# Keys of the first four tiles from LN(x)·(1 + scale), the shift added later as a bias, with a new load order and a new written order

## The chip, the cores and the metric

The kernel runs on one core of one Trainium2 chip. That core has TensorE (PE in the profile, with its weight loads listed as PEld), VectorE (DVE), ScalarE (ACT), GpSimd (POOL) and the SyncE queue (SP), which here issues nearly all transfers; 16 DMA engines carry them. The metric is device microseconds (us) of one execution, and lower is better. The kernel before took 242.55 us, the median of three runs (242.29 to 243.35).

## The reference

One transformer block on x, 2048 rows of 512 numbers in bf16. Each of its two layers takes a layernorm that is scaled and shifted by vectors computed from a conditioning row c:

```
mod = (silu(c) @ w_mod).reshape(1, 6, 1, 512)     # sa, ca, ga, sb, cb, gb
h = layernorm(x) * (1 + ca) + sa
q, k, v = h @ wqkv                                # 32 heads of 16
# each row s attends to rows s, s-2, ..., s-14 (8 keys, softmax over them)
x = x + ga * (attention @ wo)
h = layernorm(x) * (1 + cb) + sb
x = x + gb * ((silu(h @ w1) * (h @ w3)) @ w2)     # F = 1792
```

w_mod is 512 x 3072, so its first 512 columns give the shift sa and the next 512 the scale ca.

## The kernel before, in words

**Tiles.** x is cut into 16 tiles of 128 rows, tile T holding rows 128T to 128T+127, on 128 partitions. The first layer works on groups of tiles, `LN1 = [[0, 1], [2, 3], [4, 5, 6, 7], [8, 9, 10, 11], [12, 13, 14, 15]]` (L276). For each group `ln_stats` (L535 and on) takes mean and variance of each tile on DVE (`bn_stats`, L542, and `bn_aggr`, L543), the reciprocal root on POOL (L547, L549), and the normalized tile xn on DVE (L554). `ln_T` turns the tiles over, so that features lie on partitions: by PE transposes (L614) into PSUM for the first four groups, by a transposing DMA for the last. On the way out of PSUM, ACT (L622), or DVE for two of the first group's four pieces (L629), applies the modulation: times column `modc[:, 4 + ft]`, plus column `modc[:, ft]`. The result h (128 features x rows, four pieces ft) feeds `proj_qk` (L666, evicted by ACT at L674 for q and L675 for k) and `proj_v` (L685, evicted at L695). v goes out to DRAM and comes back gathered (`vsh`), four transfers of 256 KB a tile.

**Modulation.** `modulation(0)` computes shift and scale together: tanh of c (L456, ACT), two DVE operations that make silu(c) (L458, L460), a PE transpose (L462), a DVE copy into `csz` (L464), then 32 small matmuls (L480) in four parts, one for each 128-row piece of w_mod (256 KB each), and a DVE copy into `modc` (L491). Dummy matmuls of 512 columns (`warm`, L502) stand in between: `WARMS = (8, 3, 3, 4, 2)`, 20 in all.

**Attention and FFN.** For each tile, DVE multiplies q with eight shifted keys (L716, one instruction of 4096 elements a partition), PE sums heads (L725), DVE and ACT take the softmax, DVE multiplies gathered values with the weights (L800), PE sums them (L809) and applies wo (L833), DVE adds the residual (L837). The second layernorm takes its sums on ACT (L568, L579), and the FFN runs on PE (L849, L880, L892) with ACT and DVE behind it. FFN groups are `FFN = [[0,1],[2,3],[4,5,6,7],[8,9,10,11],[12,13],[14,15]]`.

**What sets the order.** Every operation is recorded with its engine, reads and writes. Two long lists written out by hand or by a search, ORDER and SLOTS, fix the sequence on each engine and the buffer of each pooled value. Each engine runs its list strictly in sequence and waits where an operation needs another engine's result or a buffer that is still in use. No scheduler decides anything at run time, so an instruction that waits holds up all that stand behind it on its engine. SP's list is the order of the loads:

```
for T in range(2):
    p.dma(x_sb[:, T, :], x_view[:, T, :], ("load", 1), (128, 1024), w=[vx[T]])
for t in range(KT):
    p.dma(wm_s[0][:, t, :], wm_view[:, t, 0:1024], ("load", 2), (128, 2048), w=[vwm0[t]], again=WMOD)
p.dma(x_sb[:, 2:4, :], x_view[:, 2:4, :], ("load", 27), (256, 1024), w=vx[2:4])
```

In ORDER the queue begins x0, x1, the four w_mod pieces, the k part of wqkv, x2-3, the q part, x4-7, the v part, x8-11, x12-15.

Of the kernel before, what the change touches and what calls it, by code (L numbers as in the profile page):

```python
# [10 lines left out]
P = 128  # L11
S = 2048
D = 512
# [254 lines left out]
WMOD = 120  # L268
WARMS = (8, 3, 3, 4, 2)
NVB = 6  # L270
NOB = 4
DMA_T = (4, 2)
# [3 lines left out]
LN1 = [[0, 1], [2, 3], [4, 5, 6, 7], [8, 9, 10, 11], [12, 13, 14, 15]]  # L276


def _build(p, A_x, A_wqkv, A_wo, B_w1, B_w3, B_w2, c, w_mod, out):
# [46 lines left out]
    modc = sb([P, 16], f32, "modc")  # L326
    mbase = sb([P, 8], bf, "mbase")
# [96 lines left out]
    vwq = [Val("wq"), Val("wk"), Val("wv")]  # L424
    wqkv_view = A_wqkv.rearrange("(t p) n -> p t n", p=P)
    for i in range(3):
# [23 lines left out]
    for g in range(NG):  # L450
# [13 lines left out]
    p.op("dve", lambda e: e.tensor_copy(csz[:, :, 7], bank(vpc).bitcast(bf)[:, 0:KT]), 180, ("mod", 1), r=[vpc, vcsz], w=[vcs])  # L464

    vmod = [Val("modA"), Val("modB")]
    vg = [Val("ga"), Val("gb")]

    def modulation(i):
        k = ("mod", 2 + i)  # L470
        vm = Val("ps_mod", psum)
        jlo = 8 * i

        def mm(e, ts):
            b = bank(vm)
            if ts[0] == 0:
                e.matmul(b[:, 0:8], ident[:], mbase[:], start=True, stop=False)
            for t in ts:
                for j in range(8):
                    ins = e.matmul(b[:, 0:8], wm_s[i][:, t, j * P:(j + 1) * P], csz[:, t, 7 - j:15 - j], start=False,  # L480
# [3 lines left out]
        o = None  # L484
        for ts in ([(t,) for t in range(KT)] if i == 0 else [tuple(range(KT))]):
            after = warm(WARMS[ts[0]]) if i == 0 else []
            o = p.op("pe", lambda e, ts=ts: mm(e, ts), (8 * len(ts) + (ts[0] == 0)) * 27, k,
                     r=[vwms[1]] * i + [vwm0[t] for t in ts] * (1 - i) + [vcs, vident, vbase] + wm_hold, part=[vm],
                     after=after + ([o] if o else []))
            last[0] = o  # L490
# [558 lines left out]
```

## Time and profile before

| what | value |
|---|---|
| median of three runs | 242.55 us |
| the profiled execution | 242.59 us, of which the span is 240.6 us |
| PE busy | 232.7 us, 97% of the span |
| DVE busy | 168.3 us, 70% |
| ACT busy | 157.9 us, 66% |
| first matmul of a projection (L666) | 10.42 us |
| first large DVE product (L716) | 23.35 us |
| moved by DMA | 38.33 MB, mean 159 GB/s |

Times in the profile count from the start of the span. In a group's or timeline's row, the first figures are start and length (or busy time and mean length), then engine, line, operation, output and inputs, number of instructions, and in brackets the idle time before and what ended it. In the view by stretch, each row has the stretch, its length, the busy time of PE, PEld, DVE, ACT and POOL with numbers of instructions, the granted clock, the share of the 16 DMA engines and GB/s. A busy PE counts matmuls whose ends are modelled, so the distance from one matmul's start to the next says more than the busy time. Several helpers record operations on one line; the line then stands for all uses, and the tile names tell them apart.

### The profile page before, as it was taken

How to read it: one execution, taken by the hardware profiler on the slowest of the kernel's cores; microseconds unless marked ns; L12 is line 12 of the kernel's file. 1: busy time of each engine (PE TensorE's matmuls, PEld its weight loads, DVE VectorE, ACT ScalarE, POOL GpSimd, SP SyncE). 2: the span in 40 equal slices, each digit the busy share in tenths (PEclk: the TensorE clock that was granted, in tenths of full speed). 3: DMA queues.
4: the chain of work that ended last, by engine and by line, in shares of the span. 5: the costliest groups of instructions: out<-in, count | busy, mean ns of one | idle time of the engine just before them, and what ended most of it. 6: DMA issues, size and time to landing. Idle time of an engine off the chain costs nothing.

```text
span 240.6 us, 4592 instructions
## 1 busy us (share of the span) xinstructions
PE 232.7 (97%) x1794; PEld 136.3 (57%) x1820; DVE 168.3 (70%) x287; ACT 157.9 (66%) x329; POOL 21.1 (9%) x54
## 2 busy tenths in 40 slices
PE   7989999999999999999999999999999999999995
PEld 2557644545577867664444444444474447576774
DVE  4489999999999999999999658335453224152352
ACT  2169687988999888768858988746754583422310
POOL 4254110000001000130000110001000100000000
DMA  6997999699499959696875963454302000301011
GB/s 191 354 321 226 284 227 248 188 289 346 131 243 270 280 163 226 183 315 101 236 184 166 204 196 75 100 152 45 89 15 52 3 0 3 85 24 65 3 44 45
DMA packets 44125, 38.33 MB, mean 159 GB/s; under 512 B 19512, under 2 KB 34888, under 8 KB 44104
## 3 DMA queue, kind: packets, MB, share of 16 engines
q1 hardware_dynamic: 44096, 38.04, 59.5%
q8 instruction: 14, 0.23, 0.4%
q14 instruction: 7, 0.06, 0.1%
q10 hardware_dynamic: 8, 0.00, 0.0%
HBM read 29.62 MB, written 4.21 MB: 141 GB/s over the span
## 4 chain that ended last, share of the span: by engine, by line
PE 79%; DMA 7%; ACT 5%; DVE 3%; SPq 2%; issue 2%; POOL 1%
PE pall L849 32%; PE pall L892 14%; PE pall L666 10%; PE pall L833 5%; PE pall L685 4%; DMA sb_w<-in_B_w_dram 4%; PE pall L809 3%; PE pall L725 3%; PE pall L502 3%; PE pall L880 3%; SPq L124 2%; DMA sb_h<-sb_xn 2%; DMA out_dram<-sb_o 2%; PE pall L614 1%; ACT sb_h L622 1%
## 5 line engine op out<-in xcount | busy, mean ns | idle before, releaser
L849 PE MATMUL pall<-sb_h,sb_w 128*128 128x256 bf16 (+1 forms) x666 | 102.5, 308 | 1.1 <-ACT sb_hh L859 0.4
L849 PEld LDWEIGHTS pall<-sb_h,sb_w 128*128 128x128 bf16 x672 | 64.7, 98 | 37.3 <-ACT sb_hh L859 1.5
L855 ACT ACTIVATE sb_sg<-pall 128x256 bf16<-128x256 f32 (+1 forms) x84 | 36.5, 457 | 33.3 <-PE pall L849 29.4
L892 PE MATMUL pall<-sb_w,sb_hh 128*128 128x512 bf16 x189 | 43.4, 379 | 0.6 <-issue 0.3
L716 DVE TENSOR_TENSOR sb_pq<-sb_q,sb_kT 128x4096 bf16<-128x4096 bf16 x16 | 36.5, 2283 | 0.0
L666 PE MATMUL pall<-sb_h,sb_wqkv 128*128 128x512 bf16 (+1 forms) x156 | 30.9, 336 | 1.1 <-ACT sb_h L622 0.5
L892 PEld LDWEIGHTS pall<-sb_w,sb_hh 128*128 128x128 bf16 x196 | 19.0, 98 | 21.4 <-issue 0.4
L859 ACT ACTIVATE sb_hh<-pall 128x256 bf16<-128x256 f32 (+1 forms) x56 | 26.3, 491 | 6.9 <-PE pall L849 6.7
L800 DVE TENSOR_TENSOR sb_vsh<-sb_vsh,sb_al 128x4096 bf16<-128x4096 bf16 x13 | 29.5, 2285 | 0.4 <-ACT sb_al L784 0.4
L908 DVE TENSOR_TENSOR sb_o<-pall,sb_x 128x512 bf16<-128x512 f32 (+1 forms) x18 | 11.1, 626 | 22.4 <-PE pall L892 14.3
L860 DVE TENSOR_TENSOR sb_hh<-sb_sg,sb_hh 128x256 bf16<-128x256 bf16 (+1 forms) x56 | 18.4, 352 | 11.4 <-ACT sb_hh L859 7.6
L666 PEld LDWEIGHTS pall<-sb_h,sb_wqkv 128*128 128x128 bf16 x160 | 14.6, 98 | 12.7 <-ACT sb_h L622 0.9
L863 DVE TENSOR_TENSOR sb_hh<-sb_sg,pall 128x256 bf16<-128x256 bf16 x28 | 10.9, 416 | 12.8 <-PE pall L849 11.4
L622 ACT ACTIVATE sb_h<-pall,sb_modc 128x256 bf16<-128x256 bf16 (+1 forms) x22 | 13.2, 673 | 8.8 <-DVE sb_modc L491 7.0
L574 POOL TENSOR_SCALAR sb_rs<-sb_var 128x2 f32<-128x2 f32 x8 | 3.5, 434 | 151.4 <-ACT sb_xn L568 151.4
L833 PE MATMUL pall<-sb_wo,sb_ot 128*128 128x512 bf16 x61 | 15.5, 380 | 0.3 <-issue 0.2
L599 ACT ACTIVATE sb_h<-sb_h,sb_modc 128x512 bf16<-128x512 bf16 (+1 forms) x20 | 13.2, 723 | 3.3 <-DMA sb_h<-sb_xn 3.3
L685 PE MATMUL pall<-sb_wqkv,sb_h 128*128 128x512 bf16 x59 | 15.0, 380 | 0.4 <-issue 0.2
L568 ACT ACTIVATE sb_xn<-sb_x,sb_nm 128x512 bf16<-128x512 bf16 x16 | 11.4, 714 | 5.9 <-DVE sb_nm L564 5.9
L579 ACT ACTIVATE sb_xn<-sb_x,sb_nb,sb_rs 128x512 bf16<-128x512 bf16 x16 | 12.7, 810 | 3.4 <-DVE sb_nb L576 3.4
L837 DVE SCALAR_TENSOR_TENSOR sb_x<-pall,sb_x 128x512 bf16<-128x512 f32 x16 | 10.9, 687 | 2.7 <-PE pall L833 2.6
L675 ACT ACTIVATE sb_kT<-pall 128x512 bf16<-128x512 f32 (+1 forms) x20 | 9.8, 519 | 3.5 <-PE pall L666 3.5
(84 smaller groups left out, 222.1 us busy)
## 6 DMA issues: line engine op xcount, KB each, us to landing
sb_vsh<-v_scratch_dram SPq DMA_DIRECT2D x52, 256.0 KB, 4.6
sb_w<-in_B_w_dram SPq DMA_DIRECT2D x6, 512.0 KB, 7.3
sb_vshx<-v_scratch_dram SPq DMA_DIRECT2D x12, 256.0 KB, 4.6
sb_w<-in_B_w_dram SPq DMA_DIRECT2D x6, 384.0 KB, 5.6
v_scratch_dram<-sb_v SPq DMA_DIRECT2D x16, 128.0 KB, 3.9
out_dram<-sb_o SPq DMA_DIRECT2D x14, 128.0 KB, 1.9
sb_wqkv<-in_A_wqkv_dram SPq DMA_DIRECT2D x3, 512.0 KB, 7.0
sb_x<-in_A_x_dram SPq DMA_DIRECT2D x3, 512.0 KB, 8.8
```

What stands on the lines that cost most here:

```text
L599: return e.activation(vh.at[:, ft, 0:n * P], vh.at[:, ft, 0:n * P], ACT.Identity, bias=modc[:, 8 * which + ft:8 * which + ft + 1], scale=m ...
L622: return e.activation(vh.at[:, ft, 0:n * P], b[:, j * 512:j * 512 + n * P], ACT.Identity, bias=modc[:, 8 * which + ft:8 * which + ft + 1], ...
L666: ins = e.matmul(bank(vp)[:, 0:n], wqkv[:, t, kind * D + ft * P:kind * D + (ft + 1) * P], vh.at[:, t, 0:n], start=(t == ORDER[0]), stop=(t ...
L685: ins = e.matmul(bank(vp), vh.at[:, t, tt * P:(tt + 1) * P], wqkv[:, t, 2 * D:3 * D], start=(t == ORDER[0]), stop=(t == ORDER[-1]))
L716: return e.tensor_tensor(vp.at[:], in0, in1, ALU.mult)
L800: return e.tensor_tensor(v_w, v_w, a_w, ALU.mult)
L833: ins = e.matmul(bank(vy), vt.at[:, ft, :], wo[:, ft, :], start=(ft == 0), stop=(ft == KT - 1))
L849: ins = e.matmul(bank(vp)[:, 0:n], wt[:, t, fi * P:(fi + 1) * P], vh.at[:, t, 0:n], start=(t == 0), stop=(t == KT - 1))
L855: p.op("act", lambda e: e.activation(vt.at[:, 0:n], bank(vgp)[:, 0:n], ACT.Silu), c_act(n), k, r=[vgp], w=[vt], table="silu")
L859: p.op("act", lambda e: e.activation(vh_.at[:, 0:n], bank(vup)[:, 0:n], ACT.Copy), c_act(n), k, r=[vup], w=[vh_])
L860: p.op("dve", lambda e: e.tensor_tensor(vh_.at[:, 0:n], vt.at[:, 0:n], vh_.at[:, 0:n], ALU.mult), 60 + n * 69 // 128, k, r=[vt], w=[vh_], ...
L892: ins = e.matmul(bank(vz), vhh[fi].at[:, tt * P:(tt + 1) * P], w2[:, fi, :], start=(fi == 0), stop=(fi == NF - 1))
```

## The change

The shift is separated from the scale for tiles 0 to 3. With hs = LN(x)·(1 + ca), the keys are (hs + sa) @ Wk = hs @ Wk + sa @ Wk, so k is computed from hs, and the column kb = sa @ Wk is added when k leaves PSUM. q and v still use hs + sa, which DVE adds before them. In parts:

- Tiles 0 to 3 are one group. `first_keys` evicts their transposes times the scale only (ACT two pieces, DVE two, for each pair of tiles), and computes k in four PSUM banks of 512 columns: tiles 0-1 piece by piece, then tiles 2-3. q of the four tiles takes matmuls of 512 columns in place of 256.
- `scales` uses the scale half of the first w_mod piece alone (17 small matmuls in place of 33). `shifts` computes sa from the shift half (16 matmuls of one column), copies it twice, and computes kb (16 more and one copy).
- Silu(c) moves from DVE to two POOL operations, and the csz copy from DVE to ACT.
- Tile 3's mean and variance come from two ACT passes and two tiny DVE operations (`moments`). The addition of epsilon for tiles 0 and 1 moves from POOL to DVE.
- SP loads x0, x1, x2, x3 (128 KB each), the four scale pieces (128 KB each), wk in two halves, the shift half (512 KB), wq, x4-7, wv, x8-11, x12-15. Later loads have another order too: the w_o quarters go behind both gate halves, one FFN piece goes ahead of them.
- `DMA_T` counts groups, so its new value leaves tiles 12 to 15 on the transposing DMA as before.
- Dummy matmuls go from 20 to 14. ORDER and SLOTS are new throughout, so the sequence of attention and FFN on every engine differs from before as well.

```diff
-WMOD = 120
-WARMS = (8, 3, 3, 4, 2)
+WMOD = 66
+WARMS = (8, 1, 1, 1, 3)
-DMA_T = (4, 2)
+DMA_T = (3, 2)
+KEV = (0, 1, 2, 3)
+STACT = (3,)
-LN1 = [[0, 1], [2, 3], [4, 5, 6, 7], [8, 9, 10, 11], [12, 13, 14, 15]]
+LN1 = [[0, 1, 2, 3], [4, 5, 6, 7], [8, 9, 10, 11], [12, 13, 14, 15]]
...
-    for T in range(2):
+    for T in range(4):
         p.dma(x_sb[:, T, :], x_view[:, T, :], ("load", 1), (128, 1024), w=[vx[T]])
...
-        p.dma(wm_s[0][:, t, :], wm_view[:, t, 0:1024], ("load", 2), (128, 2048), w=[vwm0[t]], again=WMOD)
-    p.dma(x_sb[:, 2:4, :], x_view[:, 2:4, :], ("load", 27), (256, 1024), w=vx[2:4])
+        p.dma(wm_s[0][:, t, D:2 * D], wm_view[:, t, D:2 * D], ("load", 2), (128, 1024), w=[vwm0[t]], again=WMOD)
...
+    for i in range(2):
+        p.dma(wqkv[:, i::2, D:2 * D], wqkv_view[:, i::2, D:2 * D], ("load", 4), (256, 1024), w=[vwq[1][i]])
+    vwsa = Val("wms0_sa")
+    p.dma(wm_s[0][:, :, 0:D], wm_view[:, :, 0:D], ("load", 28), (512, 1024), w=[vwsa])
...
-    p.op("dve", lambda e: e.scalar_tensor_tensor(c4s[:], thc[:], 1.0, c4[:], op0=ALU.add, op1=ALU.mult), 180, k,
-         r=[vthc, vcT], w=[vc4])
-    p.op("dve", lambda e: e.tensor_scalar(c4s[:], c4s[:], 0.5, None, op0=ALU.mult), 180, k, w=[vc4])
+    p.op("pool", lambda e: e.tensor_scalar(thc[:], thc[:], 1.0, None, op0=ALU.add), 250, k, w=[vthc])
+    p.op("pool", lambda e: e.tensor_tensor(c4s[:], thc[:], c4[:], ALU.mult), 300, k, r=[vthc, vcT], w=[vc4])
...
-    p.op("dve", lambda e: e.tensor_copy(csz[:, :, 7], bank(vpc).bitcast(bf)[:, 0:KT]), 180, ("mod", 1), r=[vpc, vcsz], w=[vcs])
+    p.op("act", lambda e: e.activation(csz[:, :, 7], bank(vpc).bitcast(bf)[:, 0:KT], ACT.Copy, scale=0.5), 180, ("mod", 1),
+         r=[vpc, vcsz], w=[vcs])
...
+        p.op("pe", lambda e: columns(e, vm, wm_s[0], lambda t: csz[:, t, 7:8]), 16 * 27, k, r=[vwsa, vcs] + wm_hold, w=[vm])
+        p.op("dve", lambda e: e.tensor_copy(sab[:], bank(vm)[:, 0:KT]), 100, k, r=[vm], w=[vsab])
+        p.op("dve", lambda e: e.tensor_copy(modc[:, 0:4], bank(vm)[:, 0:KT]), 100, k, r=[vm], w=[vsa])
+        p.op("pe", lambda e: columns(e, vb, wqkv[:, :, D:2 * D], lambda t: sab[:, t:t + 1]), 16 * 27, ("mod", 12),
+             r=[vsab] + vwq[1] + qkv_hold, w=[vb])
+        p.op("dve", lambda e: e.tensor_copy(kb[:], bank(vb)[:, 0:KT]), 100, ("mod", 12), r=[vb], w=[vkb])
...
+    def moments(T):
...
+        p.op("act", lambda e: e.activation(vn.at[:], x_sb[:, T, :], ACT.Identity, accum_out=sx[:, T, :]), c_act(512) + 212, k,
+             r=[vx[T]], w=[vs, vn])
+        p.op("dve", lambda e: e.tensor_scalar(nm[:, T, :], sx[:, T, :], -D ** -1.5, None, op0=ALU.mult), C_TINY, k, r=[vs], w=[vb])
+        p.op("act", lambda e: e.activation(vn.at[:], x_sb[:, T, :], ACT.Square, bias=nm[:, T, :], scale=D ** -0.5,
+                                           accum_out=mv[:, T, 1:2]), c_act(512) + 212, k, r=[vx[T], vb], w=[vv, vn])
...
+    def first_keys(vnss):
...
+                        if half:
+                            return e.tensor_scalar(vo.at[:, ft, c0:c0 + n], src, sc, None, op0=ALU.mult)
+                        return e.activation(vo.at[:, ft, c0:c0 + n], src, ACT.Copy, scale=sc)
...
+                if ft in KEV:
+                    return e.activation(dst, bank(vps[ft]), ACT.Identity, bias=kb[:, ft:ft + 1])
...
+        for ft in ORDER:
+            def add(e, ft=ft):
+                return e.tensor_scalar(vh.at[:, ft, :], vo.at[:, ft, :], modc[:, ft:ft + 1], None, op0=ALU.add)
...
-    modulation(0)
+    scales()
     warm(WARMS[4])
+    shifts()
     for gi, Ts in enumerate(LN1):
-        vns = [v for pr in ([[T] for T in Ts] if gi == 0 else pairs(Ts)) for v in ln_stats(pr)]
-        vh = ln_T(0, gi, vns)
+        if gi == 0:
+            vh = first_keys([[v for T in (0, 1) for v in ln_stats([T])], ln_stats([2, 3])])
+        else:
+            vh = ln_T(0, gi, [v for pr in pairs(Ts) for v in ln_stats(pr)])
```

More of the change, by code (lines that the diff above doesn't have):

```diff
@@ L481, in mm @@
                                    stop=(t == KT - 1 and j == 7))
             return ins
[L484 to L490, printed above, removed]
@@ L588, in ln_T @@
         vh = Val("h", hpool)
-        vh.pieces = [Val(f"h_{ft}") for ft in range(KT)] if not which and not gi else None
+        vh.pieces = None
+        k0 = 2 * (gi + 1) if not which else 2 * gi + 2 * len(LN1) + 2
+        modv = [vmodB] if which else [vca, vsa]
         n = len(vns)
         if gi >= DMA_T[which]:
-            k = ("tr", 2 * gi + (2 * len(LN1) if which else 0))
+            k = ("tr", k0)
             vt = Val("hT")
@@ L923, in _build @@
          ("mod", 6), r=[vwo, vg[0]], w=[vsc_wo], lock=True)
-    modulation(1)
+    modulation()
     gate(1)
```

145 lines of the change are left out of this document (110 added, 35 removed), and 128 rows, old and new, of tables (ORDER, SLOTS).

## The prediction

> **What bounds the kernel now.** I read the page's busy times, then the busy times by stretch, then the start of the chain of waits, then the order of time around the first projections and around the multiplication with the values. All figures are us unless marked.
>
> ```profile
> PE 232.7 (97%) x1794; PEld 136.3 (57%) x1820; DVE 168.3 (70%) x287; ACT 157.9 (66%) x329; POOL 21.1 (9%) x54
> ```
>
> ```profile
> 0.00:10.42 10.42, 8.61 (x61) 3.71 (x63) 4.22 (x13) 2.06 (x4) 4.24 (x21) 1.00 0.80 260
> ...
> 14.00:22.00 8.00, 7.50 (x71) 5.88 (x74) 8.00 (x25) 6.57 (x17) 4.20 (x10) 1.00 0.89 251
> 22.00:30.00 8.00, 7.79 (x103) 4.82 (x103) 8.00 (x15) 5.67 (x11) 1.09 (x3) 1.00 1.02 285
> 30.00:62.00 32.00, 31.68 (x297) 16.03 (x299) 31.80 (x33) 27.50 (x52) 1.85 (x4) 1.00 0.94 257
> 62.00:78.70 16.70, 16.32 (x155) 11.44 (x150) 16.21 (x25) 15.97 (x39) 0.99 (x2) 1.00 0.85 220
> 78.70:110.00 31.30, 30.98 (x289) 21.33 (x294) 30.25 (x53) 24.70 (x63) 3.55 (x4) 1.00 0.89 225
> 110.00:158.00 48.00, 47.42 (x297) 22.00 (x300) 37.20 (x55) 37.84 (x64) 1.85 (x4) 1.00 0.63 154
> ```
>
> TensorE (PE) is busy nearly always, so time can only come from the stretch before its first useful matmul. But from 14 to 110 VectorE (the third figure behind the length) works 94.3 of 96: a second bound, and an earlier PE helps only as far as DVE follows. The chain names what holds the start:
>
> ```profile
> 8.94 0.59 PE pall L502 x2
> 9.53 0.20 PE pall L480 x8
> 9.75 0.18 DVE sb_modc L491
> 9.95 0.73 DVE sb_h L629 x2
> ```
>
> ```profile
> 10.42 3.16 PE L666 MATMUL pall<-sb_h,sb_wqkv 128*128 128x256 bf16 x26 [0.26 <-DVE sb_h L629]
> ```
>
> Dummy matmuls (L502), the modulation (L480), its copy (L491), the first h (L629): projections begin at 10.42. The other fact is how closely DVE feeds PE:
>
> ```profile
> 56.94 4.49 DVE L800 TENSOR_TENSOR sb_vsh<-sb_vsh,sb_al 128x4096 bf16<-128x4096 bf16 x2
> 126.45 2.29 DVE L800 TENSOR_TENSOR sb_vsh<-sb_vsh,sb_al 128x4096 bf16<-128x4096 bf16 x1
> ```
>
> ```profile
> 61.72 0.60 PE L809 MATMUL pall<-sb_vsh,sb_ind 128*32 128x512 bf16 x8
> 129.00 0.60 PE L809 MATMUL pall<-sb_vsh,sb_ind 128*32 128x512 bf16 x8
> ```
>
> DVE ends at 61.43 and 128.74; PE uses the products 0.29 and 0.26 later. Shift PE alone by more and it stands waiting there.
>
> **Loads, part by part.** Landing of the four modulation pieces in the view of that tile, and the bytes moved in the first 30 us (40 slices of 0.75):
>
> ```profile
> DMA to landing us min/median/max: 3.4/3.7/4.7
> ```
>
> ```profile
> GB/s 0 0 91 291 179 229 369 361 354 350 317 380 378 355 345 352 354 351 348 347 348 310 216 296 281 111 178 239 165 251 352 231 253 369 287 268 296 268 262 276
> ```
>
> The last piece is issued at 3.1 and lands at 7.8; the 1 MB takes 4.4 from x1's landing at 3.4, 238 GB/s; other loads run at 350. Now x2 and x3 (256 KB) go first: landed near 4.2. Each piece halves to 128 KB in as many packets: between 0.37 (350 GB/s) and 1.1 (time per packet unchanged). I take 0.55, the bytes at that stretch's own rate, plus 0.4 for its slow start: the last scale piece lands at 6.9 (6.1 to 8.6). Then the k halves (256 KB each) 7.7 and 8.4, the shift half (512 KB at 238) 10.6, wq 12.1, x4-7 13.6, wv 15.1 (14.6 before: the same 3.5 MB stand ahead of it), x8-11 16.6. The w_o quarters, moved behind the gate halves, and the FFN pieces in another order are not used before 47; the queue has about the same bytes ahead of the last w1/w3 piece, so I cost it nothing; PE waits 0.2 for one at 78.5 today, and that cover is thin.
>
> **Start of PE.** Six dummies of 0.427 end at 4.06 as L502's rows have it. c4s moves to POOL: two operations, bounded by L547's 0.23 and L549's 0.58 each, ending between 3.5 and 4.2 after tanh at 2.97: hidden by the dummies but for 0.1. The csz copy on ACT (0.18 as on DVE, to 0.31 as tanh) lies under two dummies. Then scale piece, dummy, piece, tile 0's four transposes at the half rate of these rows (0.43), dummy, piece, dummy, last piece: 7.7. On DVE: bn_stats 0.67 and bn_aggr 0.18 for x0 and x1 from 2.95, two new 0.16 additions, xn0 by 5.6, two tiny operations for tile 3, whose moments ACT takes (0.72 and 0.19 each, like L568), x2's statistics to 6.85, xn1 to 7.3. xn1 also waits for tile 0's transposes (its buffer); behind it stand the modc copy and all that follows. Modc 8.0, tile 1's transposes 8.2, first DVE eviction 0.36: k starts at 8.65 against 10.42.
>
> **To the values.** From 8.65: 16 k matmuls at 0.109 (L666's spacing), 8 transposes 0.45, shift columns 16 in 0.38 (like L518's), 8 k matmuls 0.87, k bias 16 in 0.38: 3.83, so 12.5; the shift half (10.6, wanted at 11.0) and wq (12.1) arrive 0.4 ahead. Then q, 16 at 0.216, and 8 k: 4.33; v, 16 at 0.216, and 16 transposes: 4.35; together 21.2. Before, the same point is 23.65 (the chain's L685 ends at 23.77 with two transposes more). It is reached without the 1.1 of gaps that PE shows between 10.16 and 17. **PE's lead: 2.5.** ACT's evictions for q and k become 8 of 0.52 instead of 16 of 0.33 (start to start): lighter. The bias form costs 0 to 0.3 each (L675 to L579); v's banks wait for them, with about 1 us to spare.
>
> **DVE.** Removed: 0.49 for c4s, 0.18 csz, 0.75 for tile 3's statistics: 1.4. Added: two additions 0.32, two tiny 0.34, two evictions 0.73, three copies 0.51, four additions of sa (unknown; between L554's spacing of 0.32 and its 0.38; I take 0.38): 1.5. Net +2.0. Against that, before 13.45 DVE is idle 7.2 (0.96, 1.55, 0.52, 0.79, 2.25 before L491, 1.15 before L554); walking on, DVE evicts to 9.0, makes xn2 and xn3 to 9.76, evicts tiles 2-3 from 10.15 to 10.9, copies the shift at 11.45 and adds sa from 11.95 to 13.45; the new idle up to there is 4.3 (0.96, 1.5 until x0 lands, 0.5 for the last scale piece, 0.25 and 0.4 for transposes, 0.55 for the shift, little else). Lead at equal work: 7.2 - 4.3 - 2.0 = 0.9. That is the floor of the gain while DVE is full, and 2.5 the ceiling. The order decides between: adding rows from 13.45 (2.20 per large product, 0.59 bn_stats, 0.32 xn, 0.6 per softmax step), the product for tile 11, the last tight one, ends 1.1 earlier than by the same sum before, at 126.5, or at 127.6 if the 1.1 that DVE really lost on the way (0.48 and 0.30 near 103 and 108, the rest small) is lost again. PE needs 0.3 more work before it. With PE 0.26 behind, PE's gain there is 129.3 less 126.8 to 127.9: 1.4 to 2.5. After it DVE has slack (37.2 of 48). I take 1.8, a little below the middle, because the old order too lost its 1.1 there. The profiled execution took 242.59, 240.6 of it span, 0.04 above the median of 242.55: **240.8**.
>
> **Rivals.** (a) All of PE's lead is kept: 242.6 - 2.5 = 240.1. For it, FFN matmuls can stand in for late products; against it, 0.26 of room. (b) DVE takes it back: gain 0.9 or less, 241.7. For it, DVE's 94.3 of 96. (c) The clock. L502's matmuls follow each other at 0.427 until 7.4 and at 0.216 after (the clock column says 1.00 throughout). The change has 14 dummies for 20 and lets PE wait for pieces. If half rate lasts through the first 16 k matmuls and 8 transposes, 2.2 of work takes 4.4: lead 0.3, time 242.3. Against it, the waits before 7.4 sum to 0.5. The Trainium skill (TensorE: Matmul & The Clock Gate, "Part 1: The HAM clock gate") says that the clock opens after a busy window of about 3.4 us that runs free of the kernel. Missing one window would, as an estimate by that page, leave half rate to 10.8 and cost half of what lies behind 8.65, 1.1: 241.9; the one switch at 7.4 doesn't contradict it. (d) Slower: the second layernorm of tiles 4-7. In the new order PE has 13.9 of rows between their last output projection and the first FFN matmul that needs their h, against 20.7 before. The chain there was 105.13 (the last residual) to 116.4 (L599's end), 11.3, plus 1.6 for projection and residual: 12.9. But two 256 KB value loads (1.5 at 350 GB/s) now stand between the transposes in SP's queue, and a transpose issued at 30.36 among such loads landed 6.5 later against a median of 2.6. PE waits when the chain passes 13.9; at 15.7 the gain is gone; at 17 or more it is slower by over 0.5%. One 6.5 landing and those 1.5 make 18.3, a wait of 4.4: 245.2. Against it: the same four took 7.6 from first issue to last landing before, and with the 1.5 alone the chain is 14.4, a wait of 0.5 that the forecast can hold.
>
> **How the numbers follow.** Forecast 0.50 (own range 240.1 to 241.4), (a) 0.10, (b) 0.17, (c) 0.08, (d) 0.15. A measurement here can tell about 0.5%, 1.2, from no change: faster is below 241.3. Faster 0.57 (the forecast but for 0.03, and (a)), same 0.28 ((b), (c), 0.03), slower 0.15. The range reaches from the ceiling with a little more of the old gaps gone, 239.7, to 242.9, behind (c); it leaves (d) out.
>
> **What would show it.** Right: first k matmul at 8 to 9.3; v of tiles 0-3 done near 21; the first large product (L716 before) at 18.5 to 20 instead of 23.35; DVE without gaps from 14 to 103; PE waiting on the value products for 0.5 to 1.5 in all. Wrong: k after 9.8 (pieces at the slow end), spacing of 0.213 behind 9, DVE waiting for the shift half, or a PE gap of over 1 ahead of the third FFN group.

## The result and the profile after

The changed kernel takes 245.09 us, the median of six runs (244.31 to 246.22), against 242.68 for the kernel before beside it (242.21 to 243.35): 1.0100 of its time, 95% interval 1.0071 to 1.0129. It is 1% slower; 240.8 was forecast. Its profiled execution took 245.03 us, 243.0 of it span. Here and below the ratios leave out executions over 1.5% above the fastest of the same kernel, which the medians in us count, and of three kernels below (the old start, both edits, the v stores earlier) the profile caught one of these, so that only their times are used.

The busy times of the changed kernel, from its page:

```profile
PE 232.6 (96%) x1789; PEld 134.1 (55%) x1814; DVE 169.1 (70%) x295; ACT 158.3 (65%) x324; POOL 23.0 (9%) x54
```

VectorE (DVE) has 0.8 us more work than before, TensorE (PE) nothing that shows. The place of the loss is in the view by stretch, here for the kernel before and then for the changed kernel. The columns are the stretch, its length, the busy time of PE, PEld, DVE, ACT and POOL, the clock, the share of the DMA engines and GB/s.

```profile
0.00:16.00 16.00, 13.79 (x105) 7.61 (x108) 8.65 (x26) 5.19 (x11) 6.00 (x26) 1.00 0.91 291
16.00:60.00 44.00, 43.02 (x404) 24.13 (x408) 43.80 (x64) 36.42 (x73) 6.85 (x14) 1.00 0.95 258
60.00:80.00 20.00, 19.62 (x209) 13.76 (x209) 19.51 (x32) 19.27 (x46) 0.99 (x2) 1.00 0.85 225
80.00:128.00 48.00, 47.47 (x392) 28.40 (x399) 46.92 (x64) 36.42 (x79) 3.55 (x4) 1.00 0.83 207
```

```profile
0.00:16.00 16.00, 13.53 (x119) 7.66 (x121) 9.52 (x34) 6.15 (x14) 6.82 (x26) 1.00 0.83 261
16.00:60.00 44.00, 42.96 (x388) 22.78 (x394) 43.41 (x66) 36.13 (x68) 6.98 (x14) 1.00 0.93 251
60.00:80.00 20.00, 17.52 (x178) 11.19 (x180) 16.59 (x22) 16.01 (x40) 1.71 (x2) 1.00 0.82 227
80.00:128.00 48.00, 47.22 (x407) 28.65 (x403) 47.26 (x70) 38.31 (x82) 1.86 (x4) 1.00 1.02 216
```

DVE is the engine to follow, as it is full from 14 to 110 before. Up to 60 us it has done 52.93 us of work against 52.45, 0.48 more; but it has 0.86 more to do (the exact sums are 169.13 and 168.27), so at equal work it stands 0.38 us *behind* the kernel before. Between 60 and 80 it falls 2.92 further back (16.59 for 19.51), between 80 and 128 it makes up 0.34. At 128 it is 3.0 behind. After 128 us DVE has slack, and the last matmul ends 2.2 later than before (240.23 for 238.07). So the change loses in two places, a little in the start and most of it in one stretch of 20 us.

The start, on PE and then on DVE (order of time; in brackets the idle time before and what ended it):

```profile
8.87 1.03 PE L731 MATMUL pall<-sb_h,sb_wqkv 128*128 128x256 bf16 x8 [0.51 <-DMA sb_wqkv<-in_A_wqkv_dram]
...
13.35 2.32 PE L777 MATMUL pall<-sb_h,sb_wqkv 128*128 128x512 bf16 x10
...
21.96 0.55 PE L555 MATMUL pall<-sb_csz,sb_wm_g 128*128 128x1 bf16 x16
```

```profile
10.39 0.61 DVE L722 TENSOR_SCALAR sb_h<-pall,sb_modc 128x256 bf16<-128x256 bf16 x2 [1.25 <-PE pall L712]
12.02 0.16 DVE L509 CAST sb_sab<-pall 128x4 bf16<-128x4 f32 x1 [1.02 <-PE pall L505]
...
12.30 1.14 DVE L759 TENSOR_SCALAR sb_h<-sb_h,sb_modc 128x512 bf16<-128x512 bf16 x4
...
14.53 1.29 DVE L594 BATCH_NORM_STATS2 sb_st<-sb_x 128x6 f32<-128x512 bf16 x2 [0.76 <-DMA sb_x<-in_A_x_dram]
```

PE starts k at 8.87 for 10.42 and has the values of tiles 0 to 3 behind it at 21.96 (before 23.77, the L685 of the prediction). The change does what it says on PE. DVE waits three times, 3.03 us in all, where waits of 0.4 and 0.55 were forecast.

The stretch from 60 to 80, on ACT, DVE and PE:

```profile
62.41 0.60 ACT L806 ACTIVATE sb_v<-pall 128x512 bf16<-128x512 f32 x1 [2.11 <-DMA v_scratch_dram<-sb_v]
```

```profile
62.20 2.29 DVE L911 TENSOR_TENSOR sb_vsh<-sb_vsh,sb_al 128x4096 bf16<-128x4096 bf16 x1 [0.91 <-DMA sb_vsh<-v_scratch_dram]
```

```profile
63.06 1.04 PE L777 MATMUL pall<-sb_h,sb_wqkv 128*128 128x512 bf16 x4 [0.86 <-ACT sb_v L806]
64.52 0.61 PE L920 MATMUL pall<-sb_vsh,sb_ind 128*32 128x512 bf16 x8 [0.42 <-ACT sb_q L785]
71.77 1.49 PE L960 MATMUL pall<-sb_h,sb_w 128*128 128x256 bf16 x12 [0.75 <-DMA sb_w<-in_B_w_dram]
73.84 1.04 PE L944 MATMUL pall<-sb_wo,sb_ot 128*128 128x512 bf16 x4 [0.36 <-DMA sb_ot<-sb_oa]
```

Every one of these waits ends, at first or second hand, at a transfer. ACT, which works through its list in sequence, stood 2.1 us because SLOTS gives the v of tile 12, which it was to evict, the buffer of the v of tile 9, and the store of that one landed at 62.33. The buffers as such were not short: the sixth was first written at 66.67. DVE waited for the gathered values of tile 3, PE for ACT, for w3 and for a transposed output. The chain of waits of the changed kernel has two long DMA steps there which the old one has not (the old one has another, 9.70 us for a piece of w1, for which PE waits 0.16 at 78.70):

```profile
54.39 7.94 DMA v_scratch_dram<-sb_v
...
62.41 0.60 ACT sb_v L806
...
68.27 5.52 DMA sb_ot<-sb_oa
...
73.84 1.04 PE pall L944 x4
```

Why a store of 128 KB takes 7.9 us is seen in the SyncE queue (SPq, order of time), where the transfers ahead of it stand:

```profile
43.56 0.56 SPq L124 DMA_DIRECT2D sb_vsh<-v_scratch_dram  x1
44.19 3.41 SPq L124 DMA_TRANSPOSE sb_ot<-sb_oa  x2
...
48.28 0.53 SPq L124 DMA_DIRECT2D sb_vsh<-v_scratch_dram  x1
48.85 0.59 SPq L124 DMA_DIRECT2D sb_w<-in_B_w_dram  x1
...
50.03 1.83 SPq L124 DMA_DIRECT2D sb_vsh<-v_scratch_dram  x3
51.90 0.59 SPq L124 DMA_DIRECT2D sb_w<-in_B_w_dram  x1
52.54 1.81 SPq L124 DMA_DIRECT2D sb_vsh<-v_scratch_dram  x3
54.39 1.79 SPq L124 DMA_DIRECT2D v_scratch_dram<-sb_v  x2
56.22 1.15 SPq L124 DMA_DIRECT2D sb_w<-in_B_w_dram  x2
65.18 0.52 SPq L124 DMA_DIRECT2D sb_vsh<-v_scratch_dram  x1
```

The gather of tile 3 begins at 43.56 and its other three parts come at 52.54, behind two pieces of w1 (512 and 384 KB, at 48.85 and 51.90) and the gathers of tile 2. Issue runs ahead of the transfers by then: the last part of tile 3, issued at 53.74, lands at 62.17, the store behind it, issued at 54.39, at 62.33. The Trainium skill (DMA: Bandwidth & Descriptors, "Queues, rings and completion order") says that each DMA engine takes the descriptors of a ring in ring order. The trace fits that with these two, though landings can change places: the w1 piece issued at 51.90 lands at 59.69, the gather issued behind it at 52.54 lands at 59.23. The last line of the view is the other half of the delay: from 57.4 to 65.18 the queue issues nothing. It is held by the gather of tile 5, whose buffer comes free with the value sums of tile 2, and these were late on account of the waits just shown. The w3 piece (67.64) and the output transposes (66.38, 68.27) stand behind that gather, and so they are late next. In the kernel before, the eight gathers of tiles 2 and 3 are issued one behind the other, ahead of the pieces of w3 and w1:

```profile
45.95 5.08 SPq L124 DMA_DIRECT2D sb_vsh<-v_scratch_dram  x8
...
52.72 2.71 SPq L124 DMA_DIRECT2D sb_w<-in_B_w_dram  x3
62.12 2.53 SPq L124 DMA_TRANSPOSE sb_ot<-sb_oa  x2
```

That queue stands still too, from 55.43 to 62.12, and its PE has no wait above 0.16 us between 58 and 79. So a queue that is held is not a loss by itself; it depends on what stands behind.

### The profile page after: what moved, and what is told of

The parts are those of the page before. It is cut to its first block, busy times and chain, and to the rows that moved or that the text cites. A ratio compares the mean times of both kernels' runs of the same rounds, so it can differ in the third digit from the quotient of the medians.

```text
span 243.0 us, 4593 instructions
## 1 busy us (share of the span) xinstructions
PE 232.6 (96%) x1789; PEld 134.1 (55%) x1814; DVE 169.1 (70%) x295; ACT 158.3 (65%) x324; POOL 23.0 (9%) x54
## 4 chain that ended last, share of the span: by engine, by line
PE 65%; DMA 14%; SPq 7%; ACT 6%; DVE 5%; issue 2%; POOL 1%; ACTq 0%
PE pall L960 33%; PE pall L1003 14%; SPq L124 7%; PE pall L777 5%; DMA sb_wm_g<-in_w_mod_dram 4%; DMA sb_ot<-sb_oa 4%; PE pall L944 3%; DMA v_scratch_dram<-sb_v 3%; PE pall L991 3%; PE pall L796 2%; PE pall L920 2%; DMA sb_h<-sb_xn 2%; PE pall L836 2%; ACT sb_h L653 2%; ACT sb_xn L620 1%
## 5 line engine op out<-in xcount | busy, mean ns | idle before, releaser
L966 ACT ACTIVATE sb_sg<-pall 128x256 bf16<-128x256 f32 (+1 forms) x84 | 35.0, 453 | 33.5 <-PE pall L960 25.9
L911 DVE TENSOR_TENSOR sb_vsh<-sb_vsh,sb_al 128x4096 bf16<-128x4096 bf16 x12 | 27.4, 2286 | 2.4 <-ACT sb_al L895 1.3
L777 PE MATMUL pall<-sb_h,sb_wqkv 128*128 128x512 bf16 x107 | 25.8, 379 | 1.2 <-ACT sb_v L806 0.9
L971 DVE TENSOR_TENSOR sb_hh<-sb_sg,sb_hh 128x256 bf16<-128x256 bf16 (+1 forms) x56 | 17.9, 349 | 7.3 <-ACT sb_sg L966 4.0
L626 POOL TENSOR_SCALAR sb_rs<-sb_var 128x2 f32<-128x2 f32 x8 | 4.9, 608 | 145.5 <-ACT sb_xn L620 145.5
L777 PEld LDWEIGHTS pall<-sb_h,sb_wqkv 128*128 128x128 bf16 x112 | 10.3, 98 | 12.0 <-ACT sb_v L806 1.4
L796 PE MATMUL pall<-sb_wqkv,sb_h 128*128 128x512 bf16 x61 | 15.9, 379 | 0.3 <-issue 0.2
L948 DVE SCALAR_TENSOR_TENSOR sb_x<-pall,sb_x 128x512 bf16<-128x512 f32 x16 | 10.9, 688 | 6.5 <-PE pall L944 6.5
L631 ACT ACTIVATE sb_xn<-sb_x,sb_nb,sb_rs 128x512 bf16<-128x512 bf16 x16 | 12.6, 808 | 4.1 <-DVE sb_nb L628 4.1
L620 ACT ACTIVATE sb_xn<-sb_x,sb_nm 128x512 bf16<-128x512 bf16 x16 | 11.5, 720 | 2.9 <-DVE sb_nm L616 2.7
L785 ACT ACTIVATE sb_q<-pall 128x512 bf16<-128x512 f32 x16 | 9.3, 604 | 4.4 <-PE pall L777 4.4
L594 DVE BATCH_NORM_STATS2 sb_st<-sb_x 128x6 f32<-128x512 bf16 x15 | 9.9, 676 | 2.7 <-DMA sb_x<-in_A_x_dram 2.7
```

Of the source, the lines that this page charges most:

```text
L777: ins = e.matmul(bank(vp)[:, 0:n], wqkv[:, t, kind * D + ft * P:kind * D + (ft + 1) * P], vh.at[:, t, 0:n], start=(t == ORDER[0]), stop=(t ...
L796: ins = e.matmul(bank(vp), vh.at[:, t, tt * P:(tt + 1) * P], wqkv[:, t, 2 * D:3 * D], start=(t == ORDER[0]), stop=(t == ORDER[-1]))
L911: return e.tensor_tensor(v_w, v_w, a_w, ALU.mult)
L966: p.op("act", lambda e: e.activation(vt.at[:, 0:n], bank(vgp)[:, 0:n], ACT.Silu), c_act(n), k, r=[vgp], w=[vt], table="silu")
L971: p.op("dve", lambda e: e.tensor_tensor(vh_.at[:, 0:n], vt.at[:, 0:n], vh_.at[:, 0:n], ALU.mult), 60 + n * 69 // 128, k, r=[vt], w=[vh_], ...
```

## The experiments

Two theories. **Transfers:** the new place of loads, stores and gathers in the one queue makes them land late between 60 and 80 us, whatever the start gains. **VectorE:** the start puts more on DVE than it gains, and a full DVE carries this to the end. A third is that the new written order of the engines itself is worse. All ratios are to the kernel before on the same chip, with 95% intervals; each kernel is built on the changed kernel unless it says otherwise.

**The changed kernel again.** No edit.

> The changed kernel as it is, beside the others: 244.5 to 245.5 us. Its trace shows whether the slow stretch of the load queue between 7 and 12 us (shift half at 11.38 us) and the waits at 62, 64 and 71 us come in another execution too.

Measured: 245.40, 1.0097 (1.0065 to 1.0129). PE waits 0.84, 0.42 and 0.73 between 62 and 72 for the same things, and 0.55 at 79.2 behind the late gather of tile 5; DVE is busy 16.29 of the 20 us. The loss is there again, in the same place, in other executions.

**The start of one and the order of the other.** Three kernels, ORDER and SLOTS only: the new start (up to the value projections of tile 3) with the old order behind it, the old start with the new order behind it (built on the kernel before), and the new order for its first 370 instructions, to about 50 us, with the old behind it. The edit of the first:

```diff
 ORDER: the instructions of the start, in the sequence of the changed kernel
-ORDER: its other instructions
+ORDER: the same instructions, in the sequence of the kernel before
```

> The changed start (its loads, the k from LN(x) times (1 + scale), the bias, up to the value projections of tile 3) followed by the order of the kernel before for everything else, the first gate half and the w_o quarters in the load queue included. If the later order and its transfers took the lead away, the lead of 1.7 us that the values of tiles 0 to 3 have at 22 us stays: 240.5 to 241.5 us. If the start's own work and bytes (the four shift additions, later landings of wv and of x tiles 8-15) take it away, it goes as slowly as the changed kernel: 244.5 to 245.5. If both share it, about 243.

> The start of the kernel before (its loads and k from the full h), followed by the changed kernel's order for everything else. If the later order is what costs, it loses what the changed kernel loses behind 22 us, 3.4 to 4.4 us less what the late gaps give back: 245 to 247 us, with waits of TensorE at the value evictions near 62 us and at w1/w3 near 71 us again. If the start costs it, 242 to 243 us.

> The changed kernel's order to about 50 us (53 transfers, 136 matrix steps, 86 VectorE instructions), where its lead in equal TensorE work is 0.6 us, and the order of the kernel before from there. If the changed kernel's own later order loses the time, the lead stays and the waits near 62 and 71 us are not there: 241.8 to 242.4 us. If the start and its queue set the loss, it comes in this order as well: 244 us or more. A bad joint would show as a wait of several us between 47 and 60 us.

Measured: 1.0344 (1.0308 to 1.0380), 1.0325 (1.0283 to 1.0366) and 1.0191 (1.0150 to 1.0231). The first two lie where no theory put them; the third is beyond the "244 us or more" of its second case (247.49), by 3.5 us. PE of the first one, and below it DVE:

```profile
29.27 0.39 PE L668 MATMUL pall<-sb_ident,sb_xn 128*128 128x128 bf16 x2 [5.39 <-DVE sb_xn L606]
30.77 1.15 PE L668 MATMUL pall<-sb_ident,sb_xn 128*128 128x128 bf16 x8 [1.11 <-DVE sb_xn L606]
```

```profile
22.13 2.26 DVE L827 TENSOR_TENSOR sb_pq<-sb_q,sb_kT 128x4096 bf16<-128x4096 bf16 x1
...
24.91 2.28 DVE L827 TENSOR_TENSOR sb_pq<-sb_q,sb_kT 128x4096 bf16<-128x4096 bf16 x1
...
28.51 0.70 DVE L606 TENSOR_SCALAR sb_xn<-sb_x,sb_mv,sb_rs 128x512 bf16<-128x512 bf16 x2
```

The joint costs 6.5 us at once: in the old sequence DVE makes two large products before the layernorm of the next tiles, and the old PE had matmuls to do meanwhile that the new start has already done. Behind the wait the granted clock of TensorE is 0.5 from 29.2 to 36.0, which costs more. Late by that much, the stretch from 60 to 80 has no wait of PE, which says nothing of its merit. In the third kernel, whose queue is the new one up to 50 us, the gather of tile 3 lands at 62.96 and ACT waits 2.14 for a store of v, as in the changed kernel. These kernels show that an order fits the start it was written for; they do not separate the theories.

**No additions of the shift.** The four DVE additions (L759) are left out, so q and v of tiles 0 to 3 lack the shift.

```diff
-        vh = Val("h", hpool)
+        vh = vo
...
-            p.op("dve", add, 320, ("tr", 100), r=[done[ft], done[4 + ft], vsa], w=[vh.pieces[ft]], hold=[vh, vo], lock=True)
+            vh.pieces[ft].writers = done[ft].writers + done[4 + ft].writers
```

> The changed kernel without the four additions of the shift on VectorE: q and v of the first four tiles are computed from LN(x) times (1 + scale) without the shift, so this part of the computation is left out. It takes 1.3 us from VectorE and lets q start once wq is there. If VectorE's added work is what the gain went to, 243.5 to 243.9 us. If the transfers set the waits at 62 and 71 us, a longer lead only waits longer there: 244.7 to 245.2.

Measured: 244.91, 1.0080 (1.0052 to 1.0108), 0.2% (about 0.5 us) below the changed kernel, with intervals that overlap, where the additions are 1.14 us of VectorE's work. DVE still stands 3.25 us of the 20 between 60 and 80 (16.75 busy). The additions are not the main cause.

**Eight buffers for v.** The order is the same; SLOTS gives 13 of the 16 v another buffer.

```diff
-NVB = 6
+NVB = 8
```

> The changed kernel with 8 buffers for v in place of 6, the order of all instructions the same. If the v stores that land 7.9 us after their issue near 62 us hold ScalarE for 2.1 us and through it TensorE for 0.86 and 0.42 us, those waits go and the time is 243.8 to 244.4 us; if the value gathers wait for the same stores anyway or the time is taken at the next late transfer (w1/w3 near 71 us), 244.8 to 245.2. Should the DVE work of the start be the cause, 245.1 and the same lead at each stage.

Measured: 243.64, 1.0050 (1.0023 to 1.0078), as the first theory had it. ACT's 2.1 us, and PE's 0.86 and 0.42, are gone, though the stores land as late as before (7.5 us after issue). DVE works 18.10 of the 20 us; it still waits 0.44 and 1.37 for the gathers of tiles 3 and 5. No run gave the v of tile 12 the unused sixth buffer instead, so it is not shown that more buffers were needed.

**Two w3 pieces ahead of the held gather.** In the queue:

```diff
+load w3, columns 11-13 of 14
+load w3, columns 0-3
 gather tile 5, first part (waits for the value sums of tile 2)
 transpose output of tile 2
-load w3, columns 11-13 of 14
 transpose output of tile 3
...
-load w3, columns 0-3
```

> The changed kernel with two FFN weight pieces (w3 columns 11-13 and 0-3 of 14) issued ahead of the value gather of tile 5, whose wait for the value sums of tile 2 holds the queue for 7.8 us. If the held queue makes the weights late, TensorE's 0.75 us for w3 near 71 us goes: 244.2 to 244.6 us. If the two megabyte-size loads in that place push the v stores or the gathers behind them, it is taken back: 245 or more. Should the DVE work of the start be the cause, 245.1.

Measured: 243.86, 1.0070 (1.0043 to 1.0097). PE's 0.75 for w3 is gone, its 0.78 and 0.42 near 63 us remain.

**Both edits.**

```diff
-NVB = 6
+NVB = 8
 in the queue, ahead of the first part of the gather of tile 5:
+load w3, columns 11-13 of 14
+load w3, columns 0-3
```

> Both edits together on the changed kernel: 8 buffers for v, and the two w3 pieces ahead of the gather that holds the queue. With 8 buffers alone TensorE still lost 1.2 us between 64 and 78 us, with the w3 pieces alone it lost 1.4 us at 62 to 66 us and 0.3 behind. If these are two places of one chain of late transfers, the two edits add: 241.8 to 242.6 us, 0.3% either side of the kernel before. If each edit only moves the same wait, the two are no better than the one: 243.4 to 243.9.

Measured: 243.22, 1.0028 (1.0000 to 1.0056); the two edits add in part, short of the 241.8 to 242.6 expected.

**The v stores of tiles 8 and 9 ahead of three gathers of tile 3.** In the queue:

```diff
+store v of tiles 9 and 8
 gather tile 3, three parts
-store v of tiles 9 and 8
```

> The changed kernel with the stores of the v of tiles 8 and 9 issued ahead of the last three gathers for tile 3 (768 KB) instead of behind them; 6 buffers as it was. If the stores are late for their place in a queue that is some 6 us behind, they land near 60 instead of 62.4 us, ScalarE's 2.1 us and TensorE's 0.86 and 0.42 us mostly go: 243.6 to 244.3. If the gathers of tile 3, now behind them, hold VectorE instead (0.91 us at 62 us grows), it is taken back: 244.8 to 245.3.

Measured: 244.61, 1.0067 (1.0037 to 1.0098). In microseconds that is between the two expectations, in ratio 0.3% below the changed kernel: a small gain at best.

**The k weights in one piece**, in place of two halves; and the reverse, **two halves in the kernel before**, twice.

```diff
-    for i in range(2):
-        p.dma(wqkv[:, i::2, D:2 * D], wqkv_view[:, i::2, D:2 * D], ("load", 4), (256, 1024), w=[vwq[1][i]])
+    p.dma(wqkv[:, :, D:2 * D], wqkv_view[:, :, D:2 * D], ("load", 4), (512, 1024), w=[vwq[1][0]])
```

> The changed kernel with the k weights loaded by one transfer of 512 KB in place of two of 256 KB, all else the same. In the trace of the changed kernel the two halves took 2.8 us (7.15 to 9.97), in the kernel before the one piece took 1.6 (7.79 to 9.37). If the split costs that, the piece lands near 8.8, everything behind it 0.8 to 1.2 us earlier (shift half 10.3, wq 11.9, wv 14.9), q starts at 12.4 in place of 13.35, and the time is 244.2 to 244.8 if the waits at 62 and 71 us take most of it, 243.9 at the best. If the queue is slow there for another reason, it lands at 9.8, k starts 1 us later and the time is 245.1 to 246.

> The kernel before with one thing changed: its k weights in two transfers of 256 KB instead of one of 512 KB. It measures the split by itself. If two halves take longer, the second lands at 9.9 to 10.5 in place of 9.37 us, and wq, x 4-7 and wv as much later; the time rises by 0 to 0.8 us, 242.5 to 243.3. If the split costs nothing, it lands at 9.4 and the time does not move.

> The kernel before with its k weights in two transfers, once more: it was 0.3% faster than the kernel before, while the landings were the same, and the first profile had TensorE at full speed from 4.7 in place of 7.4 us. If the two transfers bring that, 0.996 to 0.998 again, with full speed near 4.7 us in the profile; if it was the luck of one chip's runs, 1.000.

Measured: in one piece 245.73, 1.0119 (1.0084 to 1.0153), landed at 9.66. In the kernel before the second half landed at 9.46, for 9.37 in one piece. So the split costs nothing that shows. Nor is the 9.97 of the first profile a property of the kernel: in the profile of the changed kernel again the second half landed at 8.70, and in the others with this start at 9.27 to 10.45. What makes the loads differ so between executions stays open. The kernel before with halves took 0.9968 (0.9955 to 0.9982) once and 0.9991 (0.9975 to 1.0006) the second time, so no gain is shown.

**All edits together**: 8 buffers, both w3 pieces ahead, k weights in one piece, and the second half's gate columns (L555, for which PE waits 0.28 at 23.5) behind four more matrix steps. Run twice.

> The changed kernel with 8 buffers for v, the two w3 pieces ahead of the gather, the k weights in one piece, and the gate columns of the second half (which TensorE waits 0.28 us for near 23.5 us) moved behind the next five matrix steps. If late transfers explain the whole loss, this is faster than the kernel before: 241.3 to 242.2 us (0.998 to 1.0 of it). If something else than transfers takes the rest, it stays where the two edits stood: 243 to 243.5.

> The combined kernel (8 v buffers, two w3 pieces ahead of the gather, k weights in one piece, gate columns later) once more, beside these: 1.001 to 1.006 of the kernel before if the earlier 1.0033 holds on another chip; if the transfers of this order depend on the chip, as the three edits' 1.0086 suggests, it is 1.007 or more where the gather of tile 3 lands at 64 us in place of 61.5.

Measured: 243.43, 1.0033 (1.0010 to 1.0055), and 243.85, 1.0051 (1.0016 to 1.0086). By stretch, the first of them, and its longest wait of PE there:

```profile
60.00:80.00 20.00, 19.02 (x209) 13.24 (x209) 18.87 (x27) 17.82 (x43) 1.34 (x2) 1.00 1.12 280
```

```profile
69.07 1.04 PE L942 MATMUL pall<-sb_wo,sb_ot 128*128 128x512 bf16 x4 [0.92 <-DMA sb_ot<-sb_oa]
```

DVE has back 2.28 of the 2.92 us, and 1.41 (18.00 busy) in the second run. What is late now is the output transpose of tile 2, behind the two w3 pieces that were moved up.

**One w3 piece ahead, the other behind the transposes**, 8 buffers, the k weights in halves; and the same without the additions of the shift.

> The changed kernel with 8 buffers for v, one w3 piece ahead of the gather that holds the queue, the other behind the two output transposes of tiles 2 and 3 (with both ahead, the transposes landed 4.5 us after issue and TensorE waited 0.92), the k weights in halves as in the changed kernel, and the gate columns of the second half behind five more matrix steps. If late transfers explain the loss, the waits of TensorE between 60 and 80 us sum to less than 0.4 and the time is 241.8 to 242.6. If a rest remains that is not transfers, 242.9 to 243.4.

> The kernel of the three edits, with the four additions of the shift left out as well (q and v of tiles 0 to 3 without the shift). Alone on the changed kernel that took 0.4 us off, though VectorE was 1.2 us further at 24 us. If the transfers had swallowed that lead and are now out of the way, VectorE's lead of 1.1 to 1.2 us reaches the end: 240.8 to 241.7, or 0.9 to 1.2 below the kernel of the three edits. If VectorE's place does not set the end at all, less than 0.4 below it.

Measured: 1.0086 (1.0054 to 1.0118) and 1.0117 (1.0078 to 1.0156), neither in a range that was expected, and not apart from each other beyond their intervals. DVE of the first, then the stretches 16 to 60 and 60 to 80 of the first and of the second:

```profile
64.55 2.29 DVE L911 TENSOR_TENSOR sb_vsh<-sb_vsh,sb_al 128x4096 bf16<-128x4096 bf16 x1 [2.11 <-DMA sb_vsh<-v_scratch_dram]
```

```profile
16.00:60.00 44.00, 42.99 (x392) 23.18 (x397) 42.71 (x65) 36.45 (x68) 6.96 (x14) 1.00 0.95 248
60.00:80.00 20.00, 16.81 (x157) 11.15 (x155) 16.02 (x19) 16.22 (x40) 2.23 (x2) 1.00 1.02 250
```

```profile
16.00:60.00 44.00, 43.00 (x381) 22.69 (x386) 42.06 (x67) 34.87 (x64) 6.96 (x14) 0.98 0.91 239
60.00:80.00 20.00, 18.81 (x171) 12.30 (x170) 17.41 (x21) 18.15 (x44) 0.92 (x2) 1.00 0.99 266
```

The gather of tile 3, in the same place as ever, landed at 64.5 on this chip, not 62, and with buffers to spare DVE took the whole wait. The gather of tile 5 now had a w3 piece among its parts and landed at 77.8. The pair says more than its times, because the profiled execution of the second came late by chance: its shift half landed at 12.56 (11.50 in the first), the granted clock was 0.5 from 14.4 to 17.8, and its first large product began at 21.98 (20.05). Up to 60 us DVE of the second has done 49.45 of work (7.39 and 42.06) against 51.96 (9.25 and 42.71): with the 1.05 that was left out (the difference of their sums), it is 1.46 behind. By 80 us they have 66.86 and 67.98 done, and with the same 1.05 they are level to 0.1. The one lost what it was ahead, waiting for gathers that landed at the same time in both (64.5 for tile 3, 77.8 and 77.9 for tile 5). In this pair of executions the transfers set the time, not where DVE stood when it got there, as the first theory says.

**The two w1 pieces behind the gathers.** Queue order alone; 6 buffers. The second kernel also has both w3 pieces ahead and the gate columns later.

```diff
 gather tile 2, first part
-load w1, columns 4-7
 store v of tile 7
 gather tile 2, three parts
-load w1, columns 11-13
 gather tile 3, three parts
 store v of tiles 9 and 8
+load w1, columns 4-7
+load w1, columns 11-13
```

> The changed kernel with one thing moved: two w1 pieces (512 and 384 KB) that stand among the gathers for tiles 2 and 3 go behind those gathers and behind the v stores of tiles 8 and 9. In all ten traces of the changed order the last gather of tile 3 lands 0.0 us before VectorE's product starts; in the kernel before it has 2.4 us to spare. If these 0.9 MB (2.5 us at 350 GB/s) take the place of the gather, it lands near 59.7 in place of 62.2, VectorE's 0.9 us and ScalarE's 2.1 us go, and the time is 243.3 to 244.2 with only 6 v buffers. If the queue is slow there whatever its order, the gather lands past 61.5 again and the time stays at 244.8 to 245.5.

> The same, with the two w3 pieces ahead of the gather of tile 5 as in the earlier run, and the gate columns of the second half behind five more matrix steps; still 6 v buffers. If late transfers are what the change lost behind 22 us, VectorE keeps its place (0.5 us behind the kernel before in equal work) to 128 us and the time is 242.3 to 243.0. If the w1 pieces, now late themselves, hold the first FFN steps near 66 us, 243.5 or more.

Measured: 244.57, 1.0071 (1.0047 to 1.0096), and 243.47, 1.0051 (1.0030 to 1.0072). DVE and ACT of the first, then PE of the second:

```profile
59.50 4.48 DVE L911 TENSOR_TENSOR sb_vsh<-sb_vsh,sb_al 128x4096 bf16<-128x4096 bf16 x2
...
75.92 2.29 DVE L911 TENSOR_TENSOR sb_vsh<-sb_vsh,sb_al 128x4096 bf16<-128x4096 bf16 x1 [1.62 <-ACT sb_xn L620]
```

```profile
61.01 0.60 ACT L806 ACTIVATE sb_v<-pall 128x512 bf16<-128x512 f32 x1 [0.21 <-PE pall L796]
```

```profile
69.58 1.04 PE L944 MATMUL pall<-sb_wo,sb_ot 128*128 128x512 bf16 x4 [1.96 <-DMA sb_ot<-sb_oa]
```

The mechanism is as the expectation had it: the gather of tile 3 lands at 58.7 with 3.0 us to spare, the two products follow each other without a wait, ACT's 2.1 us and PE's 0.86 and 0.42 are gone, with no buffer added. The size is not: the time was to be 243.3 to 244.2. The next late transfer takes most of it, the gather of tile 5 (landed at 75.8; the row names ACT, which had long been done) in the first, the output transposes behind the w3 pieces in the second.

The main kernels side by side. The ratios come from all counted executions, the other two columns from one profile each. But for the three edits, DVE's work in the stretch rises as the transfers are put right, and the time falls with it:

| kernel | ratio to before | DVE busy, 60 to 80 us | gather of tile 3 lands, product starts |
|---|---|---|---|
| before | 1 | 19.51 | 54.5, 56.9 |
| changed | 1.0100 | 16.59 | 62.2, 62.2 |
| changed, again | 1.0097 | 16.29 | 62.0, 62.0 |
| three edits | 1.0086 | 16.02 | 64.5, 64.5 |
| w1 behind the gathers | 1.0071 | 17.54 | 58.7, 61.7 |
| w3 ahead | 1.0070 | 17.63 | 62.5, 62.5 |
| w1 behind, w3 ahead | 1.0051 | 17.73 | 58.4, 60.8 |
| 8 buffers | 1.0050 | 18.10 | 61.9, 61.9 |
| all edits, two runs | 1.0033, 1.0051 | 18.87, 18.00 | 61.5, 61.5 and 62.4, 62.4 |

No version of the changed kernel is faster than the kernel before. Against the 1.0100 and 1.0097 of the changed kernel, 0.3% is no more than the intervals of two measurements allow: the moves of transfers alone (1.0067 to 1.0071) are shown by the waits that go, not by their times. Clear in time are the 8 buffers and the kernels with several edits (1.0028 to 1.0051), except for the three edits. Apart from the gate columns these edits leave the sequence on PE, DVE and ACT as it is, so the 0.5 to 0.7% that they give back was lost to the queue and the buffers, not to the new sequence.

## Why the prediction was wrong

**The step that failed most** is the one on the later queue: that the w_o quarters and FFN pieces in another order "are not used before 47; the queue has about the same bytes ahead of the last w1/w3 piece, so I cost it nothing". It asked when the moved loads are wanted. It asked nothing about what stands behind them: gathers, stores and transposes, whose results other engines need at a given time. The step measured 2.9 us of DVE between 60 and 80, of which edits to buffers and queue gave back 2.3 and 1.4 in two profiles, and 0.5 to 0.7% of the time. (The "47" is a little late too: DVE reads the w_o quarters at 42.26 in the kernel before. No wait comes of that.) The cover was called thin for the w1/w3 pieces, and one of those did come late (0.75 for 0.2); but the costly ones were the gathers of tiles 3 and 5 and the v stores, which the prediction put no price on, and the store of v that SLOTS had put in ACT's way.

**DVE's lead of 0.9** was -0.4. Idle time was to fall from 7.2 to 4.3; up to 16 us it went from 7.35 to 6.48. The eviction of tiles 2 and 3 waited 1.25 for PE's transposes (0.4 forecast), the shift 1.02 (0.55), and 0.76 for x4-7 was not foreseen. The added work was too high, not too low: +0.86 instead of +2.0, for the additions follow each other at 0.27 (1.14 for four) where 0.38 was taken, and the rows' durations overlap by 0.08. So there were two errors, of 2.0 and 1.1, with opposite signs, and the lead went with the larger one.

**Loads.** The order of landing was right, the times were 0.3 to 1.8 early, most for the second half of wk and for x8-11:

| landed at | last scale piece | wk halves | shift half | wq | x4-7 | wv | x8-11 |
|---|---|---|---|---|---|---|---|
| forecast | 6.9 | 7.7, 8.4 | 10.6 | 12.1 | 13.6 | 15.1 | 16.6 |
| measured | 7.15 | 8.74, 9.97 | 11.38 | 13.00 | 14.51 | 16.01 | 18.42 |

In two other profiles with these loads (without the additions; w1 behind, w3 ahead) the shift half landed at 10.77 and 10.72 and wq at 12.32 and 12.19, close to the forecast; in the rest they landed at 10.9 to 12.6 and 13.0 to 14.0.

**PE's start.** k at 8.65 forecast, 8.87 measured; q 12.5 and 13.35; the values done 21.2 and 21.96. PE's lead, 2.5 forecast, is 1.7 by that mark, and what is missing is the 0.85 by which q came late; ahead of it PE waited 0.51 for k weights and 0.20 for the shift half. The first large product came at 20.37 (18.5 to 20 forecast). The sum for the start was nearly right, for the engine that did not decide.

**The rivals.** (b), DVE takes the gain back, names an engine that did lose its lead at the start, but not the larger loss between 60 and 80, and not a time above the kernel before. (d) was the case on the slower side, and its mechanism, transposes behind value loads in the queue, is of the right kind; at its own place, the third FFN group, PE waited 0.49 at 118.5, which is the smaller of its two prices. The same thing 50 us earlier decided. (c), the clock: in three of the profiles used all 14 dummies run at half speed, and with 8 buffers, one of these, the first product still came at 20.41. That cost nothing that shows; the clock did cost something in the profile of the three edits without additions, where it was halved later, from 14.4 to 17.8. (a) did not come.

**The sum.** Forecast: DVE 0.9 ahead, nothing lost later, 1.8 off the time. Measured at 128 us: 0.4 behind from the start, 2.9 from the stretch, 0.3 made up, 3.0 behind, and 2.4 on the time.

What stays open: with all edits 0.3 to 0.5% remains against the kernel before. The first profile of all edits has DVE 0.4 behind from the start and 0.6 from the stretch. That this is the rest is not shown: the same execution took 242.79 us, only 0.2 above the profiled one of the kernel before. No run had every transfer in time, and the one without the additions of the shift, with its late start, did not settle whether a lead of DVE would be kept then.

## What to carry to other kernels

When transfers are reordered in a queue that is full, cost what stands *behind* the moved ones: for each gather, store or transpose there, compare its landing with the start of the instruction that needs it, and treat a few tenths of slack as none. A lead won at the start is worth only what the next resource on the way lets pass, so before pricing a start, look for the stretch where another resource sets the time. And an order searched for one program is part of that program: half of it under another start cost 2 to 3%.

## What was not expected of the hardware

- The same store (the v of tile 9), with the same transfers ahead of it from 43 us on and issued at 54.0 to 54.9, landed at 61.7 (all edits), 62.2 and 62.3 (changed kernel), and 64.7 (three edits, another chip). An order with no slack in that stretch should take such a spread in full, but the times do not show it: of the counted executions, 9 of 11 of the changed kernel and 111 of 115 of the kernel before lie within 1 us of the median of their set.
- The moment when TensorE reaches full speed moves by several us between executions of one start. Dummies of the kernels with 8 buffers, then with the w3 pieces ahead (spacing 0.43 at first; the second goes to 0.2 from 4.3 us on, while in the first all dummies are slow, and its first eight k matmuls follow at 0.21 until 10.9, against 0.11 from 11.5 on):

```profile
4.29 1.03 PE L539 MATMUL pall<-sb_ones 128*128 128x512 bf16 x2
...
8.12 1.49 PE L539 MATMUL pall<-sb_ones 128*128 128x512 bf16 x3
```

```profile
4.29 0.60 PE L539 MATMUL pall<-sb_ones 128*128 128x512 bf16 x2
...
7.92 0.81 PE L539 MATMUL pall<-sb_ones 128*128 128x512 bf16 x3
```

  The Trainium skill (TensorE: Matmul & The Clock Gate, "Part 1: The HAM clock gate") says that the window after which the clock opens runs free of the kernel, so that the number of slow matmuls differs from run to run, and that the ramp costs under 1% of a typical kernel. The traces agree: 6 to 14 slow dummies of 14, and first products at 20.41 and 20.42 in these two.
- Two transfers of 256 KB in place of one of 512 KB did not move the landing in the kernel before (9.46 and 9.28 against 9.37).
